# Cross-partition max and sum on TensorE in place of GpSimd, and the feed-forward weights first in the load stream

## Chip, cores, metric

One core of a Trainium2 chip. The metric is the device time of one execution in microseconds (us). Executions of one kernel agree mostly within 0.2%. The kernel before was timed again beside every experiment, with medians from 1325.46 to 1325.81 us, so runs of different calls can be set side by side. A kernel called faster or slower must differ by 2%; differences here are read from the intervals and from the traces.

## The reference, cut

One decode step of a block: a layer norm of one row, then cached attention with 32 heads over 32,768 positions, and a SwiGLU feed-forward beside it.

```
x: [1, 1, 640] bf16        k_cache, v_cache: [1, 32, 32768, 128] bf16 (268 MB each)
xn = layernorm(x)
q = xn @ wq                                   # 32 heads of 128
p = softmax(q . k / sqrt(128)); o = p . v     # per head, over 32768 positions
ffn = (silu(xn @ w_gate) * (xn @ w_up)) @ w_down        # 640 -> 1728 -> 640
out = x + o @ wo + ffn
```

The caches and weights are 554 MB in all, and each byte is read once.

## The kernel before

Positions of a head are spread over 128 partitions, 256 in each. K and V come in loads of 4.2 MB, two per head and cache, into a ring of six slots. VectorE multiplies K by q in place. TensorE folds the products with identity matmuls, VectorE finishes the sums. The softmax needs the maximum over all positions: VectorE reduces along each partition, GpSimd across partitions.

```python
# SyncE: loads in this order, each waits until its slot is free
units: k(0,0) k(0,1) k(1,0) v(0,0) k(1,1) v(0,1) ... k(31,1) v(30,1) ffn wo v(31,0) v(31,1)
e.dma_start(wd[:, 0:FB-1, :], B_w_down[0:(FB-1)*128, :].rearrange("(j p) n -> p j n", p=128))   # rows of 1,280 B
e.dma_start(wd[0:FL, FB-1, :], B_w_down[(FB-1)*128:F, :])
...
# GpSimd
for h in range(H):
    s = h % SR
    g.wait_ge(s_max, h + 1)
    if h >= SR:
        g.wait_ge(s_exp, h - SR + 1)
    g.partition_all_reduce(gmax[:, s:s+1], pmax[:, s:s+1], channels=128, reduce_op=ReduceOp.max).then_inc(s_g, 1)
    g.wait_ge(s_g, h + 1)
    g.tensor_scalar(out=negb[:, s:s+1], in0=gmax[:, s:s+1], scalar1=-c_scale, scalar2=None, op0=ALU.mult).then_inc(s_neg, 1)
    g.wait_ge(s_exp, h + 1)
    if h >= SR:
        g.wait_ge(s_rz, h - SR + 1)
    g.partition_all_reduce(zb[:, s:s+1], rsum[:, s:s+1], channels=128, reduce_op=ReduceOp.add).then_inc(s_z, 1)
...
# TensorE
for k in range(NK):                # NK = 64 halves of K
    scores(k)                      # 32 identity matmuls, 128x512
    h, c = divmod(k, NCH)
    if h >= 1:
        pv(h - 1, c)               # 128 matmuls, one column each
...
# ScalarE: exp(c_scale * score + negb), with its row sum in rsum
```

## Time and profile before

| | before |
|---|---|
| time, median of 4 runs | 1325.32 us (1324.44 to 1325.59) |
| DMA share, mean of the 16 engines, 60 to 1242 us | 1.00, 426 to 429 GB/s |
| PE / DVE / POOL busy | 62% / 50% / 7% |
| max on VectorE to exp on ScalarE, head 14 | about 14 us |

These are lines of the profile page of the kernel before. The DMA row is the busy share of the DMA engines in tenths, in 40 slices. `q8` are 16 KB packets that fetch instructions. The row that begins with DMA 68% is the chain that ended last. The rest are groups of instructions: count, busy time, mean, then the idle time of the engine before them and what ended it.

```profile
span 1323.6 us, 22586 instructions
...
DMA  9999999999999999999999999999999999999977
...
q8 instruction: 84, 1.38, 0.4%
...
DMA 68%; PE 16%; DVE 8%; SPq 4%; issue 3%; POOL 1%; ACT 0%; DVEq 0%; POOLq 0%
...
L241 PE MATMUL ps<-ring,ident 128*128 128x512 bf16 x2048 | 588.4, 459 | 450.7 <-DVE ring L385 450.7
L385 DVE TENSOR_TENSOR ring<-ring,qb 128x8192 bf16<-128x8192 bf16 x128 | 560.6, 4422 | 322.1 <-DMA ring<-in_A_k_cache_dram 322.1
...
L205 POOL TENSOR_SCALAR negb<-gmax 128x1 f32<-128x1 f32 x32 | 58.5, 1829 | 358.3 <-issue 358.3
L202 POOL PARTITION_ALL_REDUCE gmax<-pmax x32 | 20.0, 624 | 537.7 <-DVE pmax L400 537.7
L329 ACT ACTIVATE P<-sc,negb 128x256 bf16<-128x256 f32 x32 | 16.2, 508 | 1231.8 <-POOL negb L205 1231.8
L210 POOL PARTITION_ALL_REDUCE zb<-rsum x32 | 12.8, 400 | 295.3 <-issue 295.3
```

The DMA engines are busy in nearly every slice, and no compute engine is. Two GpSimd lines are odd. L205 (scaling the max) and L210 (the second all-reduce) sit idle for 358.3 and 295.3 us over 32 heads with the releaser "issue", that is, with nothing in the profile to wait for. That is 11.2 and 9.2 us each time. L202, the first all-reduce of a head, shows no such gap.

One of the ten windows behind the row on the DMA share (for each engine busy time and count; last three columns: granted clock, DMA share, GB/s):

```profile
532.80:651.00 118.20, 73.79 (x963) 41.67 (x962) 62.78 (x31) 2.25 (x9) 6.42 (x10) 0.73 1.00 426
```

The timeline of the kernel before, one head (start, duration, engine, operation, then the idle time before it):

```profile
597.33 0.42 DVE L400 TENSOR_REDUCE pmax<-sc 128x1 f32<-128x256 f32 x1
597.85 0.37 POOL L202 PARTITION_ALL_REDUCE gmax<-pmax  x1 [17.42 <-DVE pmax L400]
...
608.47 3.30 POOL L205 TENSOR_SCALAR negb<-gmax 128x1 f32<-128x1 f32 x1 [10.25 <-issue]
611.81 0.51 ACT L329 ACTIVATE P<-sc,negb 128x256 bf16<-128x256 f32 x1 [38.59 <-POOL negb L205]
...
621.37 0.40 POOL L210 PARTITION_ALL_REDUCE zb<-rsum  x1 [9.60 <-issue]
```

In the tail, the busy time by stretch (columns as above):

```profile
1255.00:1260.00 5.00, 0.00 (x0) 0.00 (x0) 1.22 (x1) 0.00 (x0) 0.40 (x1) 0.66 0.79 326
1260.00:1265.00 5.00, 1.74 (x5) 0.65 (x6) 5.00 (x2) 0.00 (x0) 0.00 (x0) 0.50 0.72 305
1265.00:1270.00 5.00, 5.00 (x21) 2.11 (x20) 3.23 (x2) 0.00 (x0) 0.00 (x0) 0.82 0.73 286
1270.00:1275.00 5.00, 5.00 (x134) 3.94 (x133) 1.18 (x3) 0.00 (x0) 0.37 (x1) 1.00 0.28 116
1275.00:1280.00 5.00, 0.25 (x10) 0.16 (x7) 0.00 (x0) 0.00 (x0) 0.00 (x0) 0.70 0.45 147
```

SyncE's timeline of the kernel before in the same stretch (start, duration of the issue, load):

```profile
1237.41 1.36 SPq L181 DMA_DIRECT2D ring<-in_B_w_down_dram  x1
1238.81 38.64 SPq L183 DMA_DIRECT2D ring<-in_B_w_down_dram  x1
1277.55 0.53 SPq L185 DMA_DIRECT2D ring<-in_A_wo_dram  x1
```

SyncE is held for 38.64 us at the issue of the last 64 rows of w_down, and meanwhile the DMA share falls to 0.28.

A load counts as landed when all of its engines have finished their part. The trace records 16 completions per load, one per engine. For the second V load of head 30, the last one before the tail's weights, the 16 came at these times after the first of them (us, read from the trace's completion records):

```
before   0.0 0.5 0.6 0.7 | 13.4 13.6 14.0 15.1 15.2 15.3 15.4 15.6 | 24.8 26.3 27.1 28.7    first 1239.7, last 1268.4
```

So four engines lead, eight are 13 to 16 us behind, and four are 25 to 29 us behind. At 26 us into the kernel all 16 were within 1.7 us.

### The profile page before, as it was taken

To read this page: it belongs to the slowest core of one execution; us is meant where nothing else is said; L and a number is where in the kernel's file an instruction comes from. 1 tells how busy PE (TensorE), PEld (TensorE's weight loads), DVE (VectorE), ACT (ScalarE), POOL (GpSimd) and SP (SyncE) were. 2 spreads that over 40 slices of the span, in tenths; PEclk is the share of its full clock that TensorE was granted. 3 is DMA by queue.
4 is the path that set the end of the run, shared out by engine and by line. 5 is a ranking of instruction groups with operands and counts; after the bars stand their busy time and mean duration, and the time that the engine had idled before them with its cause. 6 is when DMAs were issued, how large, how long until landed. Compare 5 with 4: busy or idle time off the path is not lost.

```text
span 1323.6 us, 22586 instructions
## 1 busy us (share of the span) xinstructions
PE 821.4 (62%) x10654; PEld 464.3 (35%) x10654; DVE 668.2 (50%) x341; ACT 31.6 (2%) x108; POOL 92.0 (7%) x102
## 2 busy tenths in 40 slices
PE   4676755755755764755765765665665665665745
PEld 1243423433423433433433433333333333333435
DVE  2765454465455464455465455465455465455430
ACT  2000000000000000000000000000000000000000
POOL 0120110000000100101000000000101000001000
PEclk9877777777777777777767767867867767866765
DMA  9999999999999999999999999999999999999977
GB/s 393 434 429 423 428 428 430 428 428 424 432 430 426 430 423 428 429 432 430 423 428 425 430 430 431 423 428 428 431 426 432 423 429 427 431 424 434 412 269 298
DMA packets 25548, 555.45 MB, mean 420 GB/s; under 512 B 2480, under 2 KB 8304, under 8 KB 8560
## 3 DMA queue, kind: packets, MB, share of 16 engines
q1 hardware_dynamic: 25456, 554.00, 98.4%
q8 instruction: 84, 1.38, 0.4%
q14 instruction: 8, 0.07, 0.0%
HBM read 553.99 MB, written 0.00 MB: 419 GB/s over the span
## 4 chain that ended last, share of the span: by engine, by line
DMA 68%; PE 16%; DVE 8%; SPq 4%; issue 3%; POOL 1%; ACT 0%; DVEq 0%; POOLq 0%
DMA ring<-in_A_k_cache_dram 68%; PE ps L241 16%; DVE ring L385 7%; SPq L183 3%; SPq L176 1%; PE ps L263 1%; POOL gmax L202 0%; POOL negb L205 0%; SPq L171 0%; DVE sc L393 0%; SPq L181 0%; ACT P L329 0%; SPq L185 0%; DVE pmax L400 0%; DVEq L381 0%
## 5 line engine op out<-in xcount | busy, mean ns | idle before, releaser
L241 PE MATMUL ps<-ring,ident 128*128 128x512 bf16 x2048 | 588.4, 459 | 450.7 <-DVE ring L385 450.7
L385 DVE TENSOR_TENSOR ring<-ring,qb 128x8192 bf16<-128x8192 bf16 x128 | 560.6, 4422 | 322.1 <-DMA ring<-in_A_k_cache_dram 322.1
L241 PEld LDWEIGHTS ps<-ring,ident 128*128 128x128 bf16 x2048 | 228.7, 114 | 785.6 <-DVE ring L385 452.8
L393 DVE TENSOR_REDUCE sc<-ps 128x64 f32<-128x512 f32 x128 | 88.5, 692 | 277.0 <-PE ps L241 277.0
L263 PEld LDWEIGHTS ps<-P,ring 128*128 128x128 bf16 x8192 | 216.4, 97 | 30.8 <-ACT P L329 10.6
L263 PE MATMUL ps<-P,ring 128*128 128x1 bf16 x8192 | 216.4, 163 | 15.5 <-ACT P L329 9.6
L205 POOL TENSOR_SCALAR negb<-gmax 128x1 f32<-128x1 f32 x32 | 58.5, 1829 | 358.3 <-issue 358.3
L202 POOL PARTITION_ALL_REDUCE gmax<-pmax x32 | 20.0, 624 | 537.7 <-DVE pmax L400 537.7
L329 ACT ACTIVATE P<-sc,negb 128x256 bf16<-128x256 f32 x32 | 16.2, 508 | 1231.8 <-POOL negb L205 1231.8
L210 POOL PARTITION_ALL_REDUCE zb<-rsum x32 | 12.8, 400 | 295.3 <-issue 295.3
L225 PE MATMUL ps<-ring,xnb 128*128 128x512 bf16 x40 | 11.1, 446 | 11.4 <-DMA ring<-in_A_wq_dram 11.4
L373 DVE RECIPROCAL rzb<-zb 128x1 f32<-128x1 f32 x32 | 4.9, 153 | 20.0 <-POOL zb L210 20.0
L400 DVE TENSOR_REDUCE pmax<-sc 128x1 f32<-128x256 f32 x32 | 13.4, 420 | 3.0
L427 DVE TENSOR_SCALAR ocol<-ps,rzb 128x1 bf16<-128x1 f32 x1 | 0.2, 221 | 25.0 <-issue 25.0
L225 PEld LDWEIGHTS ps<-ring,xnb 128*128 128x128 bf16 x40 | 4.4, 112 | 17.6 <-issue 14.5
L279 PE MATMUL ps<-xn,ring 128*128 128x1 bf16 (+1 forms) x140 | 4.4, 168 | 9.9 <-DMA ring<-in_B_w_down_dram 9.9
L294 PE MATMUL ps<-ocol,ring 128*128 128x1 bf16 x160 | 6.8, 178 | 2.5 <-DMA ring<-in_A_wo_dram 1.6
L279 PEld LDWEIGHTS ps<-xn,ring 128*128 128x128 bf16 (+1 forms) x140 | 4.3, 108 | 10.0 <-DMA ring<-in_B_w_down_dram 10.0
L294 PEld LDWEIGHTS ps<-ocol,ring 128*128 128x128 bf16 x160 | 6.6, 131 | 2.7 <-DMA ring<-in_A_wo_dram 1.7
L318 ACT ACTIVATE ocol<-ps,rzb 128x1 bf16<-128x1 f32 x31 | 7.5, 243 | 0.0
L288 PE MATMUL ps<-hcol,ring 128*128 128x1 bf16 (+1 forms) x70 | 3.0, 178 | 5.0 <-DVE hcol L420 5.0
L329 ACT ACTIVATION_READ_ACCUMULATOR P<-sc,negb 128x1 f32 x32 | 6.0, 186 | 0.0
(33 smaller groups left out, 17.5 us busy)
## 6 DMA issues: line engine op xcount, KB each, us to landing
ring<-in_A_k_cache_dram SPq DMA_DIRECT2D x64, 4096.0 KB, 45.5
ring<-in_A_v_cache_dram SPq DMA_DIRECT2D x63, 4096.0 KB, 52.3
ring<-in_A_wq_dram SPq DMA_DIRECT2D x1, 5120.0 KB, 15.0
ring<-in_A_wo_dram SPq DMA_DIRECT2D x1, 5120.0 KB, 21.6
ring<-in_B_w_gate_dram SPq DMA_DIRECT2D x1, 2160.0 KB, 23.3
ring<-in_B_w_up_dram SPq DMA_DIRECT2D x1, 2160.0 KB, 33.4
ring<-in_B_w_down_dram SPq DMA_DIRECT2D x1, 2080.0 KB, 41.8
ring<-in_A_v_cache_dram SPq DMA_DIRECT2D x1, 2048.0 KB, 21.4
```

Source lines behind the costliest of these rows:

```text
L176: e.dma_start(ring[:, s, :], kv_src(A_v_cache, h, c * CH, CH)).then_inc(s_slot[s], 16)
L183: e.dma_start(wd[0:FL, FB - 1, :], B_w_down[(FB - 1) * 128:F, :]).then_inc(s_ffn, 16)
L202: g.partition_all_reduce(gmax[:, s:s + 1], pmax[:, s:s + 1], channels=128, reduce_op=ReduceOp.max).then_inc(s_g, 1)
L205: g.tensor_scalar(out=negb[:, s:s + 1], in0=gmax[:, s:s + 1], scalar1=-c_scale, scalar2=None, op0=ALU.mult).then_inc(s_neg, 1)
L225: mm = t.matmul(bank[b], lhsT=xnb[:, c, :], rhs=wq_v[:, c, b * 512:(b + 1) * 512], start=(c == 0), stop=(c == NCD - 1))
L241: mm = t.matmul(ob, lhsT=ident[:, :], rhs=kv[:, i * HF:(i + 1) * HF, g * G:(g + 1) * G], start=(g == 0), stop=(g == DH // G - 1))
L263: mm = t.matmul(O[h % 2], lhsT=ring[:, s, j * DH:(j + 1) * DH], rhs=P[:, h % PR, jj:jj + 1], start=(jj == 0), stop=(jj == NJ - 1))
L294: mm = t.matmul(acc[:, c:c + 1], lhsT=wo_v[:, h, :, c], rhs=ocol[:, h:h + 1], start=False, stop=(h == H - 1), skip_group_check=True)
L329: a.activation(out=P[:, h % PR, :], in_=sc[:, h % SCR, :], func=ACTF.Exp, bias=negb[:, h % SR:h % SR + 1], scale=c_scale, accum_out=rsum[: ...
L385: v.tensor_tensor(out=kh, in0=kh, in1=q[:, None, :].to_broadcast([128, HF, DH]), op=ALU.mult).then_inc(s_mul, 1)
L393: v.tensor_reduce(out=sc[:, h % SCR, j:j + HF], in_=bank[n % NBK].rearrange("p (j e) -> p j e", e=G), axis=AX.X, op=ALU.add).then_inc(s_re ...
L400: v.tensor_reduce(out=pmax[:, h % SR:h % SR + 1], in_=sc[:, h % SCR, :], axis=AX.X, op=ALU.max).then_inc(s_max, 1)
```

## The change

The intent: take the 14 us of GpSimd out of every head, and take the feed-forward weights, with their small packets and the blocked issue, out of the tail. The diff, cut to its core:

```diff
-    units = []
+    units = [("wq",), ("ffn",)]
     ...
-    units += [("ffn",), ("wo",)]
+    units += [("wo",)]
-                        e.dma_start(wd[:, 0:FB - 1, :], B_w_down[0:(FB - 1) * 128, :].rearrange(
-                            "(j p) n -> p j n", p=128)).then_inc(s_ffn, 16)
+                        e.dma_start(flat[:, d0:d0 + FM * D], B_w_down[0:FM * 128, :].rearrange(
+                            "(p j) n -> p (j n)", j=FM)).then_inc(s_ffn, 16)
     # GpSimd: the whole loop over heads is removed
-                    g.partition_all_reduce(gmax..., pmax...) ; g.tensor_scalar(negb...) ; g.partition_all_reduce(zb..., rsum...)
     # TensorE, per head
+                def total(h):     # sum: ones[128,128] x rsum
+                    t.matmul(misc[:, 129:130], lhsT=ones[:, :], rhs=rsum[:, h % SR:h % SR + 1], ...)
+                def turn(h):      # the column of maxima becomes a row
+                    t.matmul(misc[0:1, 0:128], lhsT=pmax[:, h % SR:h % SR + 1], rhs=identf[:, :], ...)
+                def spread(h):    # one value to all partitions
+                    t.matmul(misc[:, 128:129], lhsT=ones[0:1, :], rhs=m1[0:1, h % SR:h % SR + 1], ...)
     # VectorE, per head, after its own reduction
+                        v.wait_ge(s_t, h + 1)
+                        v.tensor_reduce(out=m1[0:1, ...], in_=misc[0:1, 0:128], axis=AX.X, op=ALU.max)
+                        v.wait_ge(s_b, h + 1)
+                        v.tensor_scalar(out=negb[...], in0=misc[:, 128:129], scalar1=-c_scale, ...)
     # TensorE, ScalarE, VectorE: the feed-forward code moves ahead of the loop over heads (cut);
     # columns of w_gate and w_up are picked with stride 13 to match the new rows of w_down (cut)
```

## The prediction

> **What bounds the kernel now.** DMA. The page shows the 16 DMA engines 90% busy or more in 38 of 40 slices. In ten windows of 118.2 us from 60 to 1242 us (busy time by stretch) the DMA share is 1.00 each time, at 426 to 429 GB/s, while PE is busy 62%, DVE 53%, POOL 7%. The chain of waits is 68% DMA (K loads), but its 45 us waits are queueing: a freed slot only joins a queue four to five 4 MB loads deep.
>
> The page's averages hide one thing. I read each load's 16 completion increments from the trace. The Trainium skill, "DMA: Bandwidth & Descriptors", section "Why a DMA increments its semaphore by 16 and not by 1", says a load is split over up to 16 engines that finish independently; this trace agrees: the first and last engine of one load are 1.7 us apart at 26 us, 14 us at 593 us, 28.7 us at 1258 us. Four engines lag, eight are midway, four lead. Packets of 32 KB take 1.213 us everywhere, but the laggards have more stretched ones, near the 16 KB instruction fetches. The split is static, so the laggards set the end.
>
> In the tail, SyncE's issue of the last w_down piece blocks for 38.6 us (1238.8 to 1277.5, timeline), and the DMA share falls to 0.79, 0.72, 0.73, 0.28, 0.45 in five 5 us windows from 1255: about 10 us of mean engine time. But that is the leading engines running dry. The laggards carry K and V to 1268, feed-forward weights to 1285, wo to 1299, the last V to 1318.7, with no gap. So this conspicuous hole is worth nearly nothing.
>
> **What the change does.**
> - POOL: from the max (597.3) to exp (611.8) takes about 14 us per head, 32 times. Nothing waits for exp but V work done later; PE waited for it only twice (9.6 us). Off the path: about 0.
> - In its place: three fp32 matmuls of about 0.3 us (as L217) and two small DVE operations per head, with DVE waiting for PE; estimate 3.5 to 4 us from max to bias. DVE idles 322 us over 60 waits for K (5.4 each), so this fits into that idle. About 0, at worst 1 us later slot release, swallowed by the queue.
> - Feed-forward first: the same 6.5 MB, about 15 us, move from the tail to the start, where wq, feed-forward and two K loads keep the queue full for about 47 us. PE and DVE work (4.4 + 1.3 + 3 us) hides under loads at both ends. About 0.
> - w_down: 1,664 packets of 1,280 B at 0.0555 us (5.8 us per engine) become 128 of 16.6 KB (8 at 0.62 us, scaled from 17,280 B at 0.645): 0.8 us saved, on the path.
> - The tail: wo keeps its 4,096 packets of 1,280 B; the V load behind it is blocked now (14.2 us) and will be again, longer, about 35 to 40 us from the wo issue. The hole stays, and stays harmless.
>
> **Prediction.** 1325.2 - 0.8, and up to 1 us less: 1324.0 us; range 1319 to 1327. Faster by over 2%: 0.01; within 2%: 0.98; slower by over 2%: 0.01.
>
> **What would show it.** Right: steady DMA share still 1.00 at about 428 GB/s; max to exp down to about 4 us with no gain; a DMA hole after the wo issue, SyncE blocked at the next V load; the spread again near 28 us before the tail; last V landing about 1318. Wrong: a laggard engine with a gap in the old tail that the new order closes (then up to 10 us faster); or DVE waiting on PE so long that slots come free late and the steady share falls below 1.00 (slower).

## The result and the profile after

| | before | after |
|---|---|---|
| time, median of 4 runs | 1325.32 us | 1312.05 us (1311.78 to 1312.33) |
| ratio, 95% interval | | 0.9901 (0.9884 to 0.9918) |
| DMA share and rate, 60 to 1242 us | 1.00, 426 to 429 GB/s | 1.00 to 1.01, 429 to 431 GB/s |
| last engine behind the first, second V load of head 30 | 28.7 us | 17.6 us |
| last piece of the last V load landed | 1318.7 us | 1305.7 us |

The change gained 13.3 us. The prediction was 1324.0 us with a range from 1319 to 1327, so the time fell outside the range, though within the 2% that it gave 98%.

The page of the changed kernel, the lines that answer to those above:

```profile
span 1310.3 us, 22786 instructions
...
DMA  9999999999999999999999999999999999999987
...
q8 instruction: 85, 1.39, 0.4%
...
DMA 73%; PE 17%; DVE 8%; SPq 1%; issue 0%; DVEq 0%
...
L235 PE MATMUL ps<-ring,ident 128*128 128x512 bf16 x2048 | 585.8, 457 | 417.9 <-DVE ring L439 417.9
L439 DVE TENSOR_TENSOR ring<-ring,qb 128x8192 bf16<-128x8192 bf16 x128 | 560.7, 4422 | 206.4 <-DMA ring<-in_A_k_cache_dram 206.4
...
L368 ACT ACTIVATE P<-sc,negb 128x256 bf16<-128x256 f32 x32 | 16.2, 507 | 1214.6 <-DVE negb L462 1214.6
L462 DVE TENSOR_SCALAR negb<-ps 128x1 f32<-128x1 f32 x32 | 5.1, 158 | 56.8 <-PE ps L286 56.8
```

PE and DVE work is the same or a little more, and VectorE waits less for K (206.4 us in place of 322.1). The chain is still loads. The window of the steady part that answers to the one above:

```profile
532.80:651.00 118.20, 77.39 (x978) 44.26 (x978) 63.66 (x36) 1.63 (x7) 0.00 (x0) 0.72 1.00 430
```

The busy share is the same, since a stretched packet counts as busy for longer; only the rate differs. The timeline of one head shows the new path from the max to exp:

```profile
1237.79 0.42 DVE L454 TENSOR_REDUCE pmax<-sc 128x1 f32<-128x256 f32 x1
1238.53 0.38 PE L280 MATMUL ps<-identf,pmax 128*1 128x128 f32 x2
...
1238.95 0.28 DVE L457 TENSOR_REDUCE m<-ps 1x1 f32<-1x128 f32 x1 [0.74 <-PE ps L280]
1240.59 0.58 PE L286 MATMUL ps<-m,ones 1*128 1x1 f32 x2
...
1241.20 0.16 DVE L462 TENSOR_SCALAR negb<-ps 128x1 f32<-128x1 f32 x1 [1.97 <-PE ps L286]
1241.39 0.51 ACT L368 ACTIVATE P<-sc,negb 128x256 bf16<-128x256 f32 x1 [39.51 <-DVE negb L462]
```

From the start of the max (1237.79) to exp (1241.39) it is 3.6 us; the median of the heads is 3.35 us. The tail still has a hole, now behind wo, as the changed kernel's busy time by stretch shows:

```profile
1265.00:1270.00 5.00, 4.01 (x10) 1.50 (x11) 5.00 (x2) 0.00 (x0) 0.00 (x0) 0.50 0.96 369
1270.00:1275.00 5.00, 5.00 (x24) 2.21 (x22) 0.96 (x2) 0.00 (x0) 0.00 (x0) 0.96 0.54 201
1275.00:1280.00 5.00, 4.12 (x134) 3.70 (x131) 1.55 (x4) 0.65 (x3) 0.00 (x0) 1.00 0.63 224
```

And SyncE is still held, now at the V load behind wo (its timeline in the changed kernel):

```profile
1240.76 0.39 SPq L194 DMA_DIRECT2D ring<-in_A_wo_dram  x1
1255.32 24.00 SPq L184 DMA_DIRECT2D ring<-in_A_v_cache_dram  x1
```

All of that was forecast. What was not is the lag of the engines. The completions of the same V load (us after the first):

```
before   0.0 0.5 0.6 0.7 | 13.4 13.6 14.0 15.1 15.2 15.3 15.4 15.6 | 24.8 26.3 27.1 28.7    first 1239.7, last 1268.4
after    0.0 0.2 0.2 0.5 0.7 0.9 1.2 4.0 | 15.5 15.5 15.7 15.7 15.7 15.9 16.3 17.6          first 1254.9, last 1272.5
```

The first engine is 15.2 us later in the changed kernel, which is the 15 us of feed-forward weights that now come before it. The last engine is only 4.1 us later. So the leading engines run about as before, and the last ones gained 11 us. The group of four that was 25 to 29 us behind is gone; a group of eight at 13 to 18 us is still there.

### The profile page after: what moved, and what is told of

Its sections match the earlier page's. It is cut to its first block, busy times and chain, and to the rows that moved or that the text cites. A ratio compares the mean times of both kernels' runs of the same rounds, so it can differ in the third digit from the quotient of the medians. Undisturbed runs are those within 1.5% of the kernel's fastest.

```text
span 1310.3 us, 22786 instructions
## 1 busy us (share of the span) xinstructions
PE 852.6 (65%) x10846; PEld 492.8 (38%) x10846; DVE 682.5 (52%) x405; ACT 31.6 (2%) x108; POOL 1.1 (0%) x8
## 4 chain that ended last, share of the span: by engine, by line
DMA 73%; PE 17%; DVE 8%; SPq 1%; issue 0%; DVEq 0%
DMA ring<-in_A_k_cache_dram 71%; PE ps L235 17%; DVE ring L439 8%; DMA ring<-in_A_v_cache_dram 2%; SPq L184 0%; SPq L179 0%; SPq L189 0%; DVE sc L447 0%; PE ps L257 0%; SPq L191 0%; DVEq L435 0%; SPq L188 0%; DVE pmax L454 0%; SPq L187 0%; SPq L170 0%
## 5 line engine op out<-in xcount | busy, mean ns | idle before, releaser
L439 DVE TENSOR_TENSOR ring<-ring,qb 128x8192 bf16<-128x8192 bf16 x128 | 560.7, 4422 | 206.4 <-DMA ring<-in_A_k_cache_dram 206.4
L257 PE MATMUL ps<-P,ring 128*128 128x1 bf16 x8192 | 221.3, 163 | 5.7 <-DMA ring<-in_A_v_cache_dram 5.2
L462 DVE TENSOR_SCALAR negb<-ps 128x1 f32<-128x1 f32 x32 | 5.1, 158 | 56.8 <-PE ps L286 56.8
L457 DVE TENSOR_REDUCE m<-ps 1x1 f32<-1x128 f32 x32 | 8.9, 279 | 23.6 <-PE ps L280 23.6
L219 PE MATMUL ps<-ring,xnb 128*128 128x512 bf16 x40 | 11.0, 444 | 11.7 <-DMA ring<-in_A_wq_dram 11.7
L286 PE MATMUL ps<-m,ones 1*128 1x1 f32 x64 | 14.5, 293 | 0.4 <-DVE m L457 0.4
L274 PEld LDWEIGHTS ps<-rsum,ones 128*128 128x128 f32 x64 | 12.3, 194 | 4.5
L280 PE MATMUL ps<-identf,pmax 128*1 128x128 f32 x64 | 12.1, 271 | 1.2 <-DVE pmax L454 1.2
L286 PEld LDWEIGHTS ps<-m,ones 1*128 1x128 f32 x64 | 11.8, 228 | 1.2 <-DVE m L457 0.7
L427 DVE RECIPROCAL rzb<-ps 128x1 f32<-128x1 f32 x32 | 5.1, 158 | 13.6 <-PE ps L274 13.6
L295 PE MATMUL ps<-xn,ring 128*128 128x1 bf16 (+1 forms) x140 | 8.7, 198 | 5.0 <-DMA ring<-in_B_w_down_dram 5.0
L295 PEld LDWEIGHTS ps<-xn,ring 128*128 128x128 bf16 (+1 forms) x140 | 8.6, 161 | 5.5 <-issue 5.4
```

The source lines that it names most:

```text
L219: mm = t.matmul(bank[b], lhsT=xnb[:, c, :], rhs=wq_v[:, c, b * 512:(b + 1) * 512], start=(c == 0), stop=(c == NCD - 1))
L257: mm = t.matmul(O[h % 2], lhsT=ring[:, s, j * DH:(j + 1) * DH], rhs=P[:, h % PR, jj:jj + 1], start=(jj == 0), stop=(jj == NJ - 1))
L274: t.matmul(misc[:, 129:130], lhsT=ones[:, :], rhs=rsum[:, h % SR:h % SR + 1], start=True, stop=True).then_inc(s_z, 1)
L280: t.matmul(misc[0:1, 0:128], lhsT=pmax[:, h % SR:h % SR + 1], rhs=identf[:, :], start=True, stop=True).then_inc(s_t, 1)
L286: t.matmul(misc[:, 128:129], lhsT=ones[0:1, :], rhs=m1[0:1, h % SR:h % SR + 1], start=True, stop=True).then_inc(s_b, 1)
L295: mm = t.matmul(misc[0:n, off + j:off + j + 1], lhsT=hidden(w, c, j), rhs=xn[:, c:c + 1], start=(c == 0), stop=(c == NCD - 1))
```

## The experiments

**The theories.** S: GpSimd keeps the code of an all-reduce and that of an ordinary scaling apart and has to load the one or the other when it changes; this happens twice per head (the first all-reduce of a head follows an all-reduce, hence no gap before L202), and the loading slows some DMA engines. The trace of the kernel before records an instruction MODIFY_POOL_CONFIG on GpSimd ahead of L205 and of L210 in each head and none ahead of L202 after the first head; I call each change of kind a switch, 64 in all. The Trainium skill, "GPSIMD Engine Reference", section 2.1 "Instruction dispatch", says that the first call to a freshly loaded kernel pays an instruction load of about 6 us "with no visible profile instruction"; the gaps here agree in kind and are 9.2 and 11.2 us. "DMA: Bandwidth & Descriptors", section "iDMA fabric — 4 AXI ports for 8 engines, asymmetric across TPBs", says that reads of HBM by GpSimd's own cores can slow a core's load stream, and, in an explanation that it marks as unconfirmed, that some DMA engines are slowed and others not; here, too, only some of the engines fall behind, but no run shows such reads. Rivals: O, the new order closed the hole in the tail. L, the 14 us from max to exp counted after all. A, the all-reduces themselves slow the loads by their work or SBUF traffic.

A first look at the traces supports S. Packets of 32 KB normally take 1.213 us. I added up what all K and V packets took beyond that, where it was more than 0.03 us, by the time since the head's max was done (us, heads 1 to 30, from the trace's packet records):

```
since max       0-4    4-8   8-16  16-22  22-40    sum
before          8.3  104.9   11.8   29.9   20.7  175.6
after           4.4   11.7    2.5    4.4   18.5   41.5
```

The stretched packets bunch 4 to 8 us and 16 to 22 us after the max, inside the two gaps of GpSimd, and most of them vanish with the gaps.

**1. The order alone.** The changed kernel with both reductions back on GpSimd.

```diff
 # on the changed kernel
+  g.partition_all_reduce(gmax, pmax, max); g.tensor_scalar(negb, gmax, -c_scale); g.partition_all_reduce(zb, rsum, add)
-  total(h); turn(h); spread(h) and the VectorE operations between them
```

> The changed kernel, but both cross-partition reductions stay on GpSimd as before; only the order (feed-forward first) and the contiguous w_down rows are left. Theory S (GpSimd switches between the all-reduce and its scaling twice per head, each switch pulls code from HBM beside the loads and holds up half of the DMA engines): the switches remain, so only about 0.8 us is gained, 1324 to 1325 us; lag between first and last engine near 28 us again before the tail. Rival O (the order closed the DMA hole in the tail): nearly the whole gain, 1312 to 1314 us.

Measured: 1322.27 us, 0.9975 (0.9962 to 0.9987); the last engine is 26.8 us behind at the V load of head 30. So the order is not where the gain is. It gained 3.5 us by the medians, though, against 0.8 expected; see run 8.

**2. The reductions alone.** The kernel before with the TensorE reductions; feed-forward last.

```diff
 # on the kernel before
-  the GpSimd loop
+  total(h), turn(h), spread(h) on TensorE, m1 and negb on VectorE, as in the change
```

> The kernel before with the reductions on TensorE and VectorE alone; feed-forward stays last, w_down as before. Theory S: the switches are gone, about 1312.5 to 1314 us, and the lag of the last engine at the last K load is about 16 us in place of 28.7; the tail hole of SyncE blocked at the w_down remainder is still there. Rival O: 1325 us.

Measured: 1312.96 us, 0.9904 (0.9891 to 0.9918). The V load of head 30 shows eight engines at 0 to 4.3 us and eight at 14.1 to 16.1. Against the kernel before, the last engine's lag fell by 12.6 us (from 28.7 to 16.1) and the time by 12.9 us, so the lag accounts for the gain. Rival O falls; the part that is left for order and w_down is 0.9 us by the medians of this kernel and the changed one.

**3. One scaling moved.** GpSimd keeps its 64 all-reduces.

```diff
 # on the kernel before
-  g.tensor_scalar(out=negb[:, s:s+1], in0=gmax[:, s:s+1], scalar1=-c_scale, ...).then_inc(s_neg, 1)
+  a.wait_ge(s_g, h + 1)
+  a.activation(out=negb[...], in_=gmax[...], func=ACTF.Copy, scale=-c_scale).then_inc(s_neg, 1)
```

> The kernel before with one edit: the scaling of the max by minus the softmax scale moves from GpSimd to ScalarE, so GpSimd runs its 64 all-reduces and nothing else. Theory S: no switch, so the gain of the whole change comes back, 1312.5 to 1314 us. Rival A (the all-reduces themselves, their SBUF traffic or work on GpSimd, slow the loads): 1324 to 1325 us, since all 64 are still there. Rival O: 1325 us. The shorter latency from max to exp (rival L) also gains here, so this run does not tell S from L.

Measured: 1313.30 us, 0.9908 (0.9892 to 0.9923). One moved instruction brings all but about 1 us of the gain, and the last engine is 16.0 us behind. The GpSimd groups of this kernel:

```profile
L202 POOL PARTITION_ALL_REDUCE gmax<-pmax x32 | 15.3, 478 | 1189.7 <-DVE rzb L373 1054.8 <-DVE pmax L400 135.0
L207 POOL PARTITION_ALL_REDUCE zb<-rsum x32 | 14.0, 437 | 32.0 <-ACT P L329 32.0
```

The "issue" gaps are gone, though 64 all-reduces are still there. Rival A is in trouble, rival L is not yet.

**4. Idle switches in the changed kernel.** A scratch column; nobody waits for it.

```diff
 # on the changed kernel, GpSimd, per head
+  g.wait_ge(s_max, h + 1)
+  g.partition_all_reduce(du1, du0, max); g.tensor_scalar(du2, du0, -c_scale)
+  g.wait_ge(s_exp, h + 1)
+  g.partition_all_reduce(du3, du0, add)
```

> The changed kernel plus, per head, an all-reduce, a scaling and an all-reduce on GpSimd over a scratch column that nobody reads or waits for. Theory S: the 64 switches are back and slow the loads: 1323 to 1325 us. Rival L (what counted was the 14 us latency from max to exp) and rival O: unchanged, 1312 us. Rival A: also slow, since the all-reduces are back; a later run with all-reduces alone tells that apart.

Measured: 1322.46 us, 0.9977 (0.9963 to 0.9990), 10.4 us slower than the changed kernel (1312.05 us; medians of different calls, here and below where runs are set against the changed kernel). The gaps are back:

```profile
L219 POOL TENSOR_SCALAR du<-du 128x1 f32<-128x1 f32 x32 | 52.9, 1654 | 354.7 <-issue 354.7
L216 POOL PARTITION_ALL_REDUCE du<-du x64 | 33.7, 527 | 857.9 <-DVE pmax L477 558.9 <-issue 299.0
```

Nothing depends on this work, so rival L falls: the latency had no part in it.

**5 and 6. Idle work without switches.** Three all-reduces per head, or three scalings.

```diff
 # on the changed kernel: as run 4, but
 5: red, red, wait exp, red           6: scale, scale, wait exp, scale
```

> The changed kernel plus three idle all-reduces per head on GpSimd (96, more than the 64 of before), with no scaling between them, so no switch. Theory S: unchanged, 1311.5 to 1313 us. Rival A (the all-reduces themselves): 1324 us or more.

Measured: 1311.66 us, 0.9895 (0.9882 to 0.9909). The all-reduces of this kernel, with no "issue" among what ended their idle time:

```profile
L216 POOL PARTITION_ALL_REDUCE du<-du x96 | 58.5, 609 | 1210.6 <-DVE pmax L477 1119.2 <-ACT P L391 88.5
```

> The changed kernel plus three idle scalings per head on GpSimd (96, three times as many as before), no all-reduce, so no switch. Theory S: unchanged, 1311.5 to 1313 us. A rival in which any GpSimd work on SBUF slows the loads: some microseconds slower.

Measured: 1311.81 us, 0.9896 (0.9883 to 0.9910). Neither differs from the changed kernel. 96 all-reduces cost nothing, 96 scalings cost nothing, 32 of one between 64 of the other cost 10 us. Rival A falls. It is the switch: after the first 12 us the traces of runs 3, 5 and 6 record no MODIFY_POOL_CONFIG at all, and that of run 4 records it at every switch.

**7. Half of the switches.** One idle instruction per head, all-reduce and scaling by turns.

```diff
 # on the changed kernel, GpSimd
+  for h in range(H): g.wait_ge(s_max, h + 1); (red if h % 2 == 0 else scale)
```

> The changed kernel plus one idle GpSimd instruction per head, an all-reduce at even heads and a scaling at odd ones: one switch per head, 32 in place of the 64 of before. Theory S with a cost in proportion to the number of switches: half of the 13 us, so 1317 to 1320 us.

Measured: 1312.32 us, 0.9900 (0.9886 to 0.9913). A miss: no cost at all, where half was expected. The trace says that the switches did slow packets: by the same count as in the table above the sum is 99.7 us, against 41.5 in the changed kernel and 185.3 in run 4. The completions of the V load:

```
after (no switch)    0.0 0.2 0.2 0.5   0.7  0.9  1.2  4.0 | 15.5 15.5 15.7 15.7 15.7 15.9 16.3 17.6
run 7 (32 switches)  0.0 0.2 0.9 1.0 | 8.5  9.5  9.5 10.4 | 15.5 15.6 15.7 15.8 15.8 15.8 16.1 17.3
run 4 (64 switches)  0.0 0.9 1.2 1.2 | 15.1 15.2 15.4 15.6 15.6 15.7 16.2 17.2 | 23.5 25.2 25.6 26.7
```

This reads as two separate lags. Eight engines are 16 us behind in all three. Switches delay four of the other eight: by 8.5 to 10.4 us with 32 of them, which nobody sees because the eight are further behind, and by 23.5 to 26.7 us with 64, which then set the end. The time follows the larger lag, not the sum. The trace does not name the engines, so that the four are always the same is argued from the sizes of the groups, and from their steady growth: half-way through run 4, at 654 us, the eight were 7.2 to 9.1 us behind and the four 12.2 to 14.0.

**8. Contiguous w_down alone.**

```diff
 # on the kernel before
-  B_w_down[0:(FB-1)*128, :].rearrange("(j p) n -> p j n", p=128)
+  B_w_down[0:FM*128, :].rearrange("(p j) n -> p (j n)", j=FM)     # and the columns of w_gate, w_up to match
```

> The kernel before with contiguous w_down rows alone; feed-forward last, reductions on GpSimd. The 1,664 small packets become 128, so SyncE should no longer be blocked for 38 us at the w_down remainder, wo is issued some 20 us sooner and the DMA hole of the tail (shares down to 0.28) should vanish or move behind wo. If the hole cost nothing, as the prediction says, the time falls by the packet saving alone, 0.5 to 1.5 us, to about 1324 us. If the hole cost its 10 us, 1314 to 1316 us.

Measured: 1324.00 us, 0.9988 (0.9974 to 1.0002). The hold at the w_down remainder is gone (0.55 us), wo is issued at 1255.45 in place of 1277.55, and the hole moves behind wo, as the busy time by stretch shows:

```profile
1265.00:1270.00 5.00, 5.00 (x17) 1.91 (x16) 3.35 (x2) 0.00 (x0) 0.00 (x0) 0.69 0.99 394
...
1280.00:1285.00 5.00, 0.22 (x4) 0.22 (x5) 0.00 (x0) 0.75 (x3) 0.26 (x1) 0.50 0.69 255
1285.00:1290.00 5.00, 5.00 (x83) 4.97 (x83) 0.00 (x0) 0.00 (x0) 0.00 (x0) 0.50 0.27 99
```

So moving the hole did not bring its 10 us, as the prediction had it; no run took the hole away altogether. The saving is 1.6 us by the medians, and its interval just reaches 1; the packets were forecast to save 0.8. With run 1 at 3.5 us, some 1.9 us of the order's effect beside GpSimd's switches is not explained (the lag differs by as much, 26.8 us in run 1 against 28.7 in run 8); it is gone when the switches are (0.9 us between run 2 and the changed kernel).

**9, 10, 11. Why half cost nothing.** Parity exchanged; full sequences at every second head; 100 switches back to back.

```diff
 # on the changed kernel, GpSimd
 9:  (red if h % 2 == 1 else scale) per head
 10: red, scale, wait exp, red at even heads only
 11: 50 times red, scale, paced by nothing
```

> The half-dose kernel again (one idle GpSimd instruction per head, 32 switches), with the parity exchanged: the all-reduce at odd heads and the scaling at even ones. The first half-dose run gained a quarter of a microsecond where 5 to 8 were expected: its trace has half of the stretched packets, but they fell on four engines that were not the last ones. Theory P (which engines a code load holds up depends on what the K and V stream is reading just then, so on the parity of the head): now four of the lagging engines are hit, 1317 to 1322 us. Theory N (the cost depends on the number of code loads and their kind alone, the same engines each time): unchanged, 1312 to 1313 us.

Measured: 1312.46 us, 0.9901 (0.9884 to 0.9917). Parity plays no part.

> The changed kernel plus the full idle sequence (all-reduce, scaling, all-reduce) at even heads only: 32 switches as in the half dose, but in 16 pairs as before. If the pairing is what hits the lagging engines: half of the 10.4 us of the full dose, 1316 to 1319 us. If it is the parity of the head: as the first half dose, 1312 to 1313 us.

Measured: 1312.46 us, 0.9902 (0.9887 to 0.9917). Pairing plays no part; four engines at 9.2 to 11.7 us, eight at 15.7 to 17.3.

> The changed kernel plus 50 all-reduces and 50 scalings in turn on GpSimd, paced by nothing: about 100 switches, one every 11 to 12 us, up to about 1220 us. Theory S with a cost that grows with the number of switches: more than the 64 of before, 1325 to 1332 us. If 64 already saturate it: 1322 to 1325 us.

Measured: 1346.61 us, 1.0165 (1.0149 to 1.0180), 34.6 us slower than the changed kernel; at 842 us four engines are already 29.4 to 33.0 us behind and the eight at 8.8 to 10.8. So 32, 64 and 100 switches cost 0, 10 and 35 us. I had expected 13 to 20 us here. Lags counted from the first engine understate run 11, where the first completion of the second V load of head 30 is itself 19.5 us later than in the changed kernel (1274.4 against 1254.9 us). Counted from 1254.9 us, the four's last completion came 10.9 us later with 32 switches, 28.3 with 64 and 52.0 with 100, which is 0.34, 0.44 and 0.52 us per switch. Above the 17.6 us of the eight this leaves nothing, 10.7 and 34.4 us, and the measured costs are 0.3, 10.4 and 34.6 us. So the threshold in time is the lag of the eight. Why the delay per switch grows, and why the leading engines came late in run 11, is open.

**12 and 13. Relieving half of the engines.** A try at a faster kernel and at the claim that the laggards set the end.

```diff
 # on the changed kernel, first piece of the last V load (2 MB)
-  one load of 128 partitions
+  12: 16 loads of 8 neighbouring partitions      13: 16 loads of 8 partitions, four apart
```

> The changed kernel with one edit in the tail: the first piece of the last V load (2 MB, 4.9 us per engine) is issued as 16 loads of 8 partitions each, which the Trainium skill says go to the eight lowest-numbered engines only. In the changed kernel eight engines lag by 16 us at the last K load. If the laggards are the high-numbered eight, they are relieved of 4.9 us: about 1307 to 1309 us, faster than both kernels. If the laggards are the low-numbered eight, they get 4.9 us more: 1316 to 1318 us. If they are mixed: about as the latter. It also tests that the end is set by the work of the laggards alone.

Measured: 1329.25 us, 1.0026 (1.0011 to 1.0041). Not 1316 to 1318, so not the forecast of either side. Packets of 16 KB in the tail took 1.4 us in the median and up to 2.0, in place of 0.61.

> The tail relief once more. In the first try the packets of the 8-partition loads took 1.5 us in place of 0.61 us per 16 KB, so the transfer itself got slow: the eight partitions of one load were neighbours. Here each load takes eight partitions four apart. If the packets are back near 0.61 us and the laggards are the high-numbered eight engines: 1307 to 1309 us, faster than both kernels. If the laggards are the low-numbered eight: 1316 to 1318 us. If the packets stay slow, the try says nothing about the engines again.

Measured: 1320.30 us, 0.9959 (0.9942 to 0.9975). Half of the packets took under 0.7 us, but the slowest tenth 1.2 us, twice the normal. Both runs are inconclusive about which engines lag. That such a load goes to eight engines, as the Trainium skill states ("DMA: Bandwidth & Descriptors", section "Why a DMA increments its semaphore by 16 and not by 1"), agrees with both traces: their 16 loads left 144 records of completion, 16 while they were issued and 128 later, eight per load. Which eight, the traces do not say. They show that loads of 8 partitions are slow.

**14, 15. What holds the eight back.** More TensorE instructions, and a control with more columns in few instructions.

```diff
 # on the changed kernel, TensorE, per half of K
+  14: 64 matmuls of 1 column (4,096 in all)       15: 8 matmuls of 256 columns (512 in all)
```

> The changed kernel with 64 one-column matmuls more per K half on TensorE, 4,096 in all, into unused PSUM columns that nobody reads: about 8,200 instructions more on a stream of 22,800. Theory F (the eight engines that still lag by 16 us in the changed kernel are held up by the fetches of the instruction stream, of which the trace records 85 packets of 16 KB): about 115 such packets, the lag grows by a third, the time by 4 to 7 us, 1316 to 1319 us. Rival: the lag has another cause, 1312 us.

Measured: 1317.79 us, 0.9942 (0.9925 to 0.9958). The lag of the eight rose from 15.5 to 17.6 us to 21.6 to 22.2.

> Control for the run before it: 8 matmuls of 256 columns per K half, about the same TensorE time, but only 512 matmuls in all. Theory F: about 89 fetch packets, 1312 to 1313 us. If TensorE time is what counts, as much slower as the run with many small ones.

Measured: 1312.05 us, 0.9899 (0.9884 to 0.9913), the changed kernel's time. The instruction fetches on the page of run 14 (packets, MB, share):

```profile
q8 instruction: 117, 1.92, 0.6%
```

And on the page of run 15:

```profile
q8 instruction: 89, 1.46, 0.5%
```

So 32 fetch packets of 16 KB more than the changed kernel's 85 cost 5.7 us: 0.70 us per thousand instructions (5.74 us over 8,192). The control was weaker than meant: its matmuls kept TensorE busy for 66.3 us, those of run 14 for 111.5 us. A cost in proportion to that time would have been 3.4 us, and none was seen; the 0.7 us that the slope gives for its four more fetches was not seen either. The packet records point to the fetches too: between 60 and 1242 us, 78 of the changed kernel's 83 stretched K and V packets lie within 0.3 us of a fetch packet, and 112 of 113 in run 14. In the kernel before it is 160 of 609, and of the other 449, 438 overlap a gap of GpSimd after a switch, where 57% of all such packets do.

**16, 17. The other direction, and a faster kernel.** VectorE folds once before TensorE does; the changed kernel again on the same chip.

```diff
 # 16, on the changed kernel
-  TensorE: 16 identity matmuls per half of 64 positions
+  VectorE: kh[:, :, 0:64] += kh[:, :, 64:128]
+  TensorE: 8 identity matmuls
```

> The changed kernel with half of the score matmuls: VectorE, which is idle 48% of the time, first adds the upper half of each product row to the lower (64 columns in place of 128), so TensorE folds 1,024 times in place of 2,048. About 2,000 TensorE instructions fewer. The run with 4,096 small matmuls more cost 5.7 us for 8,192 instructions, 0.70 us per thousand. Theory F: the same slope downwards, 1.4 us less than the changed kernel, 1310.2 to 1311.2 us, about 77 fetch packets, lag near 15 us. If TensorE or VectorE work bounded anything, VectorE's extra 2.2 us per half would cost time instead, 1313 us or more.

Measured: 1310.41 us, 0.9887 (0.9872 to 0.9902).

> The changed kernel once more, unaltered, on the same chip as the run before it, so that 1 us can be told: 1311.7 to 1312.4 us.

Measured: 1312.13 us, 0.9899 (0.9883 to 0.9916). The page of run 16:

```profile
span 1308.7 us, 20866 instructions
...
PE 621.5 (47%) x9822; PEld 388.1 (30%) x9822; DVE 960.8 (73%) x533; ACT 31.6 (2%) x108; POOL 1.1 (0%) x8
...
q8 instruction: 77, 1.26, 0.4%
```

It is 1.7 us faster than the changed kernel beside it, against 1.4 expected, its result is correct, and it is ahead of both kernels, by 1.7 us for VectorE at 73% and PE at 47% (65% in the changed kernel). The two ranges of run times do not overlap (1310.38 to 1310.70 and 1311.92 to 1312.22).

## Why the prediction was wrong

- **What bounds the kernel: right.** The DMA share stayed at 1.00, and the laggards of the DMA engines set the end. The Trainium skill's statement that a load's engines finish independently ("DMA: Bandwidth & Descriptors", "Why a DMA increments its semaphore by 16 and not by 1") is what led to the lag, and the trace agrees (28.7 us between first and last).
- **The hole in the tail: right.** Runs 2 and 8: with the old hole kept, the gain came all the same; with the hole moved, it did not. A kernel without a hole was not tried.
- **Latency off the path, TensorE operations for nothing: right.** 3.3 us from max to bias, median of the heads, against 3.5 to 4 forecast, and no gain from that (run 4 lost 10.4 us with the short path in place).
- **w_down 0.8 us: in keeping with the runs**, which cannot tell it exactly: 0.9 us between run 2 and the changed kernel, 1.6 us in run 8.
- **The step that failed** is "POOL: from the max (597.3) to exp (611.8) takes about 14 us per head, 32 times. Nothing waits for exp but V work done later; [...] Off the path: about 0." GpSimd was weighed by who waits for it. Its cost was what it did to the loads while nobody waited: 64 switches went with four DMA engines 25 to 29 us behind, 9 to 13 us further than the next group, and those four set the end. Removing the switches alone gained 12.5 us (run 3, by the medians).
- **The sign that was misread.** The prediction says that the laggards' stretched packets lie "near the 16 KB instruction fetches". That holds for the group of eight (runs 14 to 16). It was taken for all twelve. The four last had a second cause, and the two unexplained "issue" gaps of 358.3 and 295.3 us on GpSimd pointed to it. Sorting the stretched packets by the time since the max, as above, would have pointed to it before any run.
- **Its own test caught it:** it named a lag "near 28 us" and a last landing "about 1318" as signs of being right; they were 17.6 and 1305.7 us.

What is shown and what is argued: that the switches cost the time, and that they stretch K and V packets at the moment of the gaps, is shown. That the stretching comes from code read out of HBM beside the loads is argued from the skill and from the timing; no record of the trace shows these reads. The instruction fetches are not it: the page counts 84 of their packets before and 85 after.

## What to carry to other kernels

On a kernel bound by its loads, ask of every engine not only who waits for it but what it fetches: an idle gap with no releaser on GpSimd can go with slower DMA engines, here probably through a code load. Where a loop alternates all-reduces and scalings on GpSimd, try it with one kind alone; moving one scaling to another engine brought nearly the whole gain of this change. And since a load is as late as its slowest engine, compare the 16 completions of a load early and late: the lags of different groups of engines did not add here, so a cost can stay hidden until it passes the largest of the others.

## What the Trainium skill lacked or had wrong

- "GPSIMD Engine Reference", section 2.1, gives about 6 us for a code load and speaks of the first call after it. Here it recurs at every change between an all-reduce and a scaling, 9.2 and 11.2 us on the mean beside a saturated load stream. The page does not say that going back and forth between kinds brings the gap each time, nor that this slows the loads: 64 switches 10.4 us, 32 nothing, 100 34.6 us.
- "DMA: Bandwidth & Descriptors", section "iDMA fabric", tells that GpSimd's own reads of HBM slow a load stream, for programs that issue such reads. It has no case in which ordinary GpSimd instructions slow the loads without the program asking for reads; here, with all-reduces and scalings in turn, four of 16 engines end 25 to 29 us behind.
- "Runtime: NRT & Kernel Launch", section "Instruction fetch mechanics", calls the cost of crossing from one 16 KiB block of instructions to the next "mostly hidden", and does not say what the refill does to loads beside it. Here it is not hidden: the lag of eight DMA engines grew with the instruction count, and 32 more refills cost 5.7 us (0.70 us per thousand TensorE instructions), 8 fewer gained 1.7 us.
- No page says how many packets a queue takes before the issuing engine is held: SyncE was held for 38.6 us behind 1,664 packets of 1,280 B, for 24.0 us behind 4,096, and for 0.55 us when the 1,664 had become 128.
